# A first part of 144 rows streamed as 192 columns in tiles of its own, in a fused attention, routing and expert kernel

## The chip, the core and the metric

The kernel runs on one core of a Trainium2 chip. A core has five engines that run side by side and meet only at semaphores: PE (TensorE, the matmuls; PEld is its weight load, which overlaps the matmuls), DVE (VectorE), ACT (ScalarE), POOL (GpSimd) and SP (SyncE, which here issues most of the transfers). The metric is the device time of one execution in microseconds. Before the change it is 773.58 us, the median of 3 runs (773.41 to 774.14). PE's clock has two levels, 2.4 GHz (granted clock 1.00) and 1.2 GHz (0.50), and the profile gives the granted clock of each stretch.

## The reference

Three pieces follow each other. Attention: 4 batches, 8 heads, 576 tokens of width 64, a pooled attention over groups of 4 tokens plus a local one over a band of 7 tokens. Its output, 2304 tokens of width 512, goes through a routed layer, and that one's output through a last layer of width 2048:

```
logits = x @ w_gate;  expert_idx = argmax(logits, axis=1)
for e in range(8):                      # w1[e]: 512 x 1024, w2[e]: 1024 x 512
    h = maximum(x[expert_idx == e] @ w1[e], 0)
    out[expert_idx == e] = gate_w * (h @ w2[e])
h = out @ w_in                          # 512 x 2048
g = where(h >= 1, h, where(h <= -1, 0, (h + 1)**2 / 4))
return g @ w_out                        # 2048 x 512
```

All of it is float32 in and out.

## The kernel before

**Precision.** A float32 operand of the two big layers is split into a high part (rounded to the type fp32r) and a low part (the rest). Each product is then three passes: high by high, low by high, high by low. `whi` makes the high part of a block of weights on ACT (names wraw to wh), `wlo` the low part (wl) on DVE or POOL. Activations are split the same way into xh and xl, hidden values into hh and hl.

**Attention and routing.** The steps of this part are written out by hand in the string ORDER: each word names a step (S, AV, xt, ...) with its numbers, and the loop at L785 emits them one after the other, which fixes the order on every engine. At its end tokens are routed in chunks of 128-row groups (CHUNKS): `lg` the logits, `ct` a transpose of them, `ch` the argmax on DVE (it writes oh_all, the one-hot choice), `gt` the gate, `ra`/`rk`/`rd` a token's place in its expert's list (PE adds up one-hot rows; dst_all is the place). `xt` transposes 128 tokens back to rows, `xm` scales them on ACT or DVE into one of four buffers xr, and `xs` scatters them with POOL to their expert's rows in the DRAM tensor xs_d.

**Slots.** The experts are handled in 8 slots, by their number of tokens, the fullest first; slot s has a capacity CAPS[s] (416 for slot 0). For eight steps f, `emit_p1` makes 128 hidden rows from the slot's tokens (12 matmuls, weights stationary, tokens streamed as columns), and `emit_p2` adds their share to four output banks y0 to y3 (12 matmuls). A block of 512 KB of weights serves two steps; eight blocks make a slot. Blocks come through 4 raw buffers (wraw), so a load waits until an earlier block is split.

**The first slot is started early.** After 9 of the 18 groups, `pick` (L652) chooses the expert that is fullest so far. `ld_rows` (step xa) then reads its first NA = 128 rows from xs_d while routing still goes on. Step XA.0 transposes them on PE, XA.1 casts them to xh on ACT, XA.2 makes xl on DVE. Steps wh.0 to wh.2 make the high parts of the slot's first three blocks, wqp.0, wqv.1 and wqv.2 their low parts (p on POOL, v on DVE), and wl.0 to wl.5 issue the loads of six blocks. With these rows alone, part A runs the first FA = 6 steps of slot 0. Part B runs the same steps for the columns from NA on, in two forms that the program chooses between by the token count: to column 416, or to NARROW[0] = 352 when the expert has no more. The inputs take the second. Then steps 6 and 7 run over all columns. Before A, `clear` zeroes PSUM banks with matmuls against a zero column, because A and B write different columns of the same bank.

**Beside A.** `count` adds up the one-hot rows on PE for the tokens per expert. `tables` (13 small DVE operations and two count matmuls) turns them into the slots' experts and counts, `starts` (8 DVE operations, after A's second step) and `positions` (4, after the third) into places in the output. Each iteration of the loop over `seq` ends with the split of the next weight block if WFIRST allows it (after the second, third and fourth step: blocks 3, 4 and 5). After the fourth step comes a branch (`emit_overflow`, not taken here), and `load_n` reads the count of slot 0 into a register of PE. `load_rest` (L839) reads the rest of slot 0's rows, after the last scatter. `x_rest` (L1036) transposes and splits them, half before and half after A's last `emit_p2`.

PSUM banks of the routing part are taken from a list by `take` in the order in which they were given back.

Of the kernel before, what the change touches and what calls it, by code (L numbers as in the profile page):

```python
# [32 lines left out]
CAP = 384  # L33
# [5 lines left out]
NWB, NWC, NWR = 3, 4, 4  # L39
NA, GA, FA, TOP = 128, 3, 6, 4096  # L40
NWT = NWB + NWC
# [45 lines left out]
nmv.11 voa.3.1 xt.10 cx.3 gt.3 aca.9.0 ap.9.0 AV.9.1 xt.9 rk.3 xt.11 tr.11 AV.10.0 aca.9.1 ap.9.1 rd.3 lg.4 xma.10  # L87
AV.10.1 xmv.9 ad.10.0 bda.11.0 xma.11 bdv.11.2 bdv.11.1 loa.4 bda.11.3 wh.0 wh.1 ct.4 ra.4 xs.10 ad.10.1 ch.4 cx.4 xt.12 xt.13 lg.5 XA.0 rk.4 gt.4 xs.11 AV.11.1 AV.11.0 rd.4 xs.9 wqp.0 wl.2 wl.3 xma.13 XA.1 loa.5 ad.11.1 ct.5 ad.11.0 xt.14 ch.5 wqv.1 wl.4 lg.6 ra.5 xma.12 wh.2 loa.6
xma.14 ct.6 rk.5 rd.5 xs.13 xt.15 cx.5 ra.6 ta gt.5 xt.17 xs.12 xs.14 xma.15 xt.16 ch.6 xs.15 cx.6 gt.6 XA.2 wl.5 rk.6 rd.6
xma.16 xma.17 xs.16 xs.17 wqv.2  # L90
"""
# [29 lines left out]
def body(ctx: ExitStack, tc: tile.TileContext, qT, kT, kD, vS, wg, w1, w2, w_in, w_out, cst, out, dbg=None, parts="all"):  # L121
# [547 lines left out]
    def next_pools():  # L669
        early.close()  # L670
        P["hp"] = pool(ctx, "hp", 3, "left")
        wC.extend(pool(ctx, f"wC{i}", NWC, "left") for i in range(2))
        P["xp"], P["xq"] = pool(mctx, "xp", 1, "left"), pool(mctx, "xq", 1, "left")

    P = {}

    def ld_rows():

        first["xr"] = P["xp"].tile([128, 4, DM], F32, tag="xr2", name="xr2")
        i_ = SP.dma_start(out=first["xr"][:, 0, :], in_=xs_d[bass.ds(sp_exp[0] * ROWS, NA), :])  # L680
        early_rows.append(i_)

    def xa_(k):
        if k == 0:
            p_ = first["p"] = take("xa")
            for c in range(4):
                PE.transpose(out=p_[:, NA * c:NA * c + NA], in_=first["xr"][:, 0, 128 * c:128 * c + 128], identity=ident)
            first["x"] = [[P["xq"].tile([128, CAPS[0]], F32R, tag=f"x{t}{c}", name=f"x{t}{c}") for t in "hl"] for c in range(4)]
        for c, (hi, lo) in enumerate(first["x"]):
            src = first["p"][:, NA * c:NA * c + NA]  # L690
# [4 lines left out]
        if k == 2:  # L695
            give("xa")

# [11 lines left out]
    def count(a, b):  # L709
        n_ps = T["n"] = T["n"] if a else take("n")  # L710
        for g in range(a, b):
            PE.matmul(out=n_ps[:, 0:E], lhsT=onesb, rhs=oh_all[:, g, :], start=(g == 0), stop=(g == NR - 1))
# [126 lines left out]
    def load_rest():  # L839
        last = SP.value_load(last_i[0:1, 0:1], min_val=0, max_val=E * ROWS - 128)  # L840
        xr, m = first["xr"], (CAPS[0] - 128 - NA) // 2
        SP.dma_start(out=xr[0:m, 1:3, :], in_=xs_d[bass.ds(sp_exp[0] * ROWS + NA, 2 * m), :].rearrange("(t p) d -> p t d", p=m))
        SP.dma_start(out=xr[:, 3, :], in_=xs_d[bass.ds(last, 128), :])

# [325 lines left out]
    for k, (v, f) in enumerate(seq):  # L1170
        if k == FA - 1:
            xb = x_rest()
            next(xb)
            emit_p2(v, f, hl, yb)
            next(xb)
            hln = emit_p1(*seq[k + 1], xhl)
        elif k + 1 < len(seq):
# [17 lines left out]
        elif k == 2:  # L1195
# [201 lines left out]
```

## Time and profile before

| | |
|---|---|
| median of 3 runs | 773.58 us |
| the profiled execution, own time | 781.72 us |
| its span, first to last instruction | 780.0 us |
| granted clock, mean over the span | 0.967 |
| PE busy | 753.1 us (97%) |
| DVE, ACT, POOL busy | 526.3, 341.3, 257.4 us |
| part A's first product to part B's start | 122.0 to 157.7 us |

The profile is of one execution, which took 8.1 us more than the median of the runs without a profile. A busy engine in it is one with an instruction in flight, so PE's 97% is not 97% of its peak. Idle time is listed with the engine that ended it.

### The profile page before, as it was taken

The page shows a single profiled execution, that of the slowest core. Times are in us where ns is not written, and L with a number is a line of the kernel's source. Part 1 is how long each engine was busy: PE and PEld are TensorE (multiplying, and loading weights), DVE is VectorE, ACT ScalarE, POOL GpSimd, SP SyncE. Part 2 cuts the span into 40 slices and gives each one's busy share as a digit, 9 for nine tenths or more (in the row PEclk, how much of TensorE's full clock was granted, in tenths as well). Part 3 has the DMA queues.
Part 4 walks back from the last instruction along what each step waited for, and adds up shares of the span by engine and source line. Part 5 has one row for each costly group of instructions (what it writes and reads, how often), then busy time and mean ns, then how long its engine had stood idle before and what let it go on. Part 6 is the DMA issues. An engine that isn't in the chain of part 4 may idle for free.

```text
span 780.0 us, 14586 instructions
## 1 busy us (share of the span) xinstructions
PE 753.1 (97%) x5667; PEld 681.5 (87%) x5668; DVE 526.3 (67%) x908; ACT 341.3 (44%) x709; POOL 257.4 (33%) x243
## 2 busy tenths in 40 slices
PE   4799989999999999999999999999999999999996
PEld 2567668999999999999999899999899899899896
DVE  5879965366466877875676676676876868744444
ACT  1767773145354565554454544333333333322221
POOL 5536653000014334300275733333323333221113
PEclk9989996589999999999999999999999999999999
DMA  9879256236456655763001011010101000011112
GB/s 287 233 245 308 96 183 214 84 118 188 152 165 218 214 191 202 243 218 110 28 28 55 28 54 54 29 55 28 55 28 55 30 25 1 1 41 40 41 42 81
DMA packets 47833, 87.11 MB, mean 112 GB/s; under 512 B 3100, under 2 KB 23964, under 8 KB 47752
## 3 DMA queue, kind: packets, MB, share of 16 engines
q1 hardware_dynamic: 44872, 76.56, 30.5%
q0 software_dynamic: 2880, 9.44, 3.2%
q8 instruction: 55, 0.90, 0.5%
q14 instruction: 26, 0.21, 0.1%
HBM read 76.55 MB, written 9.44 MB: 110 GB/s over the span
## 4 chain that ended last, share of the span: by engine, by line
PE 72%; issue 5%; POOL 2%; ACT 1%; DVE 1%; DMA 1%; POOLq 0%; SPq 0%; ACTq 0%; PEldq 0%
PE s L1136 23%; PE y L1282 15%; PE y L1086 13%; PE s L1069 12%; PE o L1282 8%; POOL out_dram L1302 1%; PE o L1022 1%; DMA xr<-xs_d 1%; ACT wh L181 0%; PE o L1042 0%; DVE wl L185 0%; POOLq L1392 0%; POOL gap_t L1304 0%; DVE hl L1009 0%; ACT hh L1008 0%
## 5 line engine op out<-in xcount | busy, mean ns | idle before, releaser
L1136 PE MATMUL s<-yT,wh 128*128 128x384 f32 x448 | 140.4, 336 | 0.0
L965 POOL TENSOR_SCALAR cvm<-cvm 128x512 f32<-128x512 f32 x32 | 52.8, 1650 | 245.6 <-ACT cvm L964 245.1
L1148 ACT CAST hh<-r 128x384 fp32r<-128x384 f32 x95 | 48.8, 513 | 161.3 <-DVE r L1144 161.3
L1143 DVE SCALAR_TENSOR_TENSOR r<-r 128x384 f32<-128x384 f32 x96 | 61.6, 642 | 64.7 <-ACT r L1142 63.2
L1142 ACT ACTIVATE r<-s,half 128x384 f32<-128x384 f32 x96 | 55.7, 580 | 87.5 <-PE s L1136 87.3
L1149 DVE TENSOR_TENSOR hl<-r,hh 128x384 fp32r<-128x384 f32 x95 | 56.4, 593 | 55.1 <-ACT hh L1148 54.0
L185 DVE TENSOR_TENSOR wl<-wraw,wh 128x1024 fp32r<-128x1024 f32 x63 | 79.6, 1279 | 18.0 <-ACT wh L181 17.3
L1136 PEld LDWEIGHTS s<-yT,wh 128*128 128x128 f32 x448 | 83.5, 188 | 4.6
L1136 PE MATMUL s<-yh,wh 128*128 128x384 f32 x256 | 86.3, 337 | 0.0
L1136 PE MATMUL s<-yh,wl 128*128 128x384 f32 x256 | 86.2, 337 | 0.0
L940 POOL TENSOR_TENSOR wl<-cvm,wh 128x512 fp32r<-128x512 f32 x32 | 51.0, 1594 | 98.5 <-ACT wh L939 87.5
L1086 PE MATMUL y<-hh,wh 128*128 128x240 f32 (+7 forms) x280 | 80.5, 309 | 0.0
L1086 PE MATMUL y<-hh,wl 128*128 128x240 f32 (+7 forms) x280 | 79.3, 304 | 0.0
L1008 ACT ACTIVATE hh<-s 128x288 fp32r<-128x288 f32 (+8 forms) x70 | 28.9, 413 | 104.1 <-PE s L1069 103.0
L1282 PE MATMUL y<-wl,hh 128*128 128x512 f32 x189 | 74.4, 393 | 0.0
L1282 PE MATMUL y<-wh,hh 128*128 128x512 f32 x189 | 73.8, 390 | 0.0
L1009 DVE SCALAR_TENSOR_TENSOR hl<-s,hh 128x288 fp32r<-128x288 f32 (+8 forms) x70 | 32.0, 457 | 58.2 <-ACT hh L1008 57.8
L181 ACT CAST wh<-wraw 128x1024 fp32r<-128x1024 f32 x64 | 65.5, 1045 | 5.4 <-issue 3.6
L1282 PE MATMUL y<-wh,hl 128*128 128x512 f32 x189 | 59.2, 392 | 0.0
L1086 PEld LDWEIGHTS y<-hh,wl 128*128 128x128 f32 x280 | 56.4, 201 | 0.0
L1086 PEld LDWEIGHTS y<-hh,wh 128*128 128x128 f32 x280 | 56.4, 201 | 0.0
L1144 DVE TENSOR_TENSOR r<-s,r 128x384 f32<-128x384 f32 x96 | 53.5, 557 | 3.3
(321 smaller groups left out, 1677.0 us busy)
## 6 DMA issues: line engine op xcount, KB each, us to landing
wraw<-in_dram SPq DMA_DIRECT2D x88, 512.0 KB
v_s<-in_dram SPq DMA_DIRECT2D x12, 512.0 KB
kbd<-in_dram SPq DMA_DIRECT2D x16, 296.0 KB
kraw<-in_dram SPq DMA_DIRECT2D x4, 1152.0 KB
craw<-in_dram SPq DMA_DIRECT2D x8, 512.0 KB
q_t<-in_dram SPq DMA_DIRECT2D x4, 768.0 KB
xr<-xs_d SPq DMA_DIRECT2D x10, 256.0 KB
q_t<-in_dram SPq DMA_DIRECT2D x4, 400.0 KB
```

The lines of the kernel that those rows point to most:

```text
L181: ACT.copy(out=hi, in_=raw)
L185: eng.tensor_tensor(out=lo, in0=raw, in1=hi.bitcast(F32), op=ALU.subtract)
L940: POOL.tensor_tensor(out=lo, in0=m, in1=hi.bitcast(F32), op=ALU.subtract)
L965: POOL.tensor_scalar(out=m, in0=m, scalar1=PAT_MIN * PAT_MIN, scalar2=None, op0=ALU.is_ge)
L1069: PE.matmul(out=h_ps[:, b:m], lhsT=w[wi][:, o:o + 128], rhs=xhl[c][xi][:, b:m], start=(n == 0), stop=(n == 11))
L1086: PE.matmul(out=y_ps[c][:, b:m], lhsT=w[wi][:, o:o + 128], rhs=hl[xi][:, b:m], start=(f == 0 and i == 0 and v not in ("A", "B")), stop=(f ...
L1136: PE.matmul(out=h_ps[:, 0:CAP], lhsT=w[wi][:, o:o + 128], rhs=yhl[j, c][xi], start=(n == 0), stop=(n == 11))
L1142: ACT.activation(out=r, in_=h_ps[:, 0:CAP], func=AF.Relu, scale=0.5, bias=half[:, 0:1])
L1143: DVE.scalar_tensor_tensor(out=r, in0=r, scalar=1.0, in1=r, op0=ALU.min, op1=ALU.mult)
L1144: DVE.tensor_tensor(out=r, in0=h_ps[:, 0:CAP], in1=r, op=ALU.max)
L1149: DVE.tensor_tensor(out=lo[:, 0:CAP], in0=r, in1=hi[:, 0:CAP].bitcast(F32), op=ALU.subtract)
L1282: PE.matmul(out=p, lhsT=gl[gi][:, 128 * t:128 * t + 128], rhs=w[wi][:, o + c:o + c + p.shape[-1]], start=(f % 4 == 0 and i == 0), stop=(f ...
```

## The change

Part A takes 144 rows instead of 128 (NA) and streams 192 columns (NZ). The 48 columns behind the rows are zeros, written once by POOL. A's operands no longer lie in the tiles of slot 0 (`first["x"]`) but in four tiles hi0 of 384 columns, one half for the high and one for the low part (`first["xa"]`). These tiles existed already for a later use and now come from another pool, allocated earlier. After A's third step ACT and POOL copy the 144 columns into `first["x"]`, for steps 6 and 7. Part B has 272 columns, or 208 in the narrow form (before 288 and 224).

The 144 rows are read as two tiles of 72 rows, so XA.0 has eight transposes of 72 columns in two PSUM banks, where it had four of 128 in one. The rest is two tiles of 72 rows and the last 128 rows.

In ORDER, wh.0 comes earlier, and the low part of block 0 moves from POOL to DVE (wqp.0 to wqv.0) to an earlier place. XA.1 and XA.2 move ahead, wqv.1 behind the routing of the last chunk, and the low part of block 2 (wqv.2) leaves ORDER and stands behind `tables` in the program. `count` takes its bank by preference from o0, o1 and s0.

```
-NA, GA, FA, TOP = 128, 3, 6, 4096
+NA, NZ, GA, FA, TOP = 144, 192, 3, 6, 4096
...
-AV.10.1 xmv.9 ad.10.0 bda.11.0 xma.11 bdv.11.2 bdv.11.1 loa.4 bda.11.3 wh.0 wh.1 ct.4 ...
+AV.10.1 xmv.9 ad.10.0 bda.11.0 xma.11 bdv.11.2 bdv.11.1 wh.0 wqv.0 loa.4 bda.11.3 wh.1 ct.4 ...
...
-    def take(*key):
-        held[key] = free.pop(0)
+    def take(*key, first=()):
+        held[key] = free.pop(min((free.index(t) for t in first if t in free), default=0))
...
         P["hp"] = pool(ctx, "hp", 3, "left")
+        hi0.extend(P["hp"].tile([128, CAP], F32R, tag=f"hi0{c}", name=f"hi0{c}", bufs=1) for c in range(4))
...
-        i_ = SP.dma_start(out=first["xr"][:, 0, :], in_=xs_d[bass.ds(sp_exp[0] * ROWS, NA), :])
+        i_ = SP.dma_start(out=first["xr"][0:NA // 2, 0:2, :],
+                          in_=xs_d[bass.ds(sp_exp[0] * ROWS, NA), :].rearrange("(t p) d -> p t d", p=NA // 2))
...
+            first["xa"] = [[hi0[c][:, i * NZ:i * NZ + NZ] for i in range(2)] for c in range(4)]
...
+            for hl in first["xa"]:
+                for t in hl:
+                    POOL.memset(t[:, NA:].bitcast(F32), 0.0)
             for c in range(4):
-                PE.transpose(out=p_[:, NA * c:NA * c + NA], in_=first["xr"][:, 0, 128 * c:128 * c + 128], identity=ident)
+                if c % 2 == 0:
+                    first["p", c // 2] = take("xa", c // 2)
+                for t in range(2):
+                    o = NA * (c % 2) + m * t
+                    PE.transpose(out=first["p", c // 2][:, o:o + m], in_=first["xr"][0:m, t, 128 * c:128 * c + 128], identity=ident[0:m, 0:m])
...
-        n_ps = T["n"] = T["n"] if a else take("n")
+        n_ps = T["n"] = T["n"] if a else take("n", first=("o0", "o1", "s0"))
...
-        return (0, 0, NA, 0) if v == "A" else (0, NA, CAPS[0], NARROW[0]) if v == "B" else (v, 0, CAPS[v], NARROW[v])
+        return (0, 0, NZ, 0) if v == "A" else (0, NA, CAPS[0], NARROW[0]) if v == "B" else (v, 0, CAPS[v], NARROW[v])
...
-    xhl = first["x"]
+    xhl = first["xa"]
...
     tables()
+    wd_(DVE, 2)
     hb[0] = bank("s0")
...
             next(xb)
+            xhl = first["x"]
             hln = emit_p1(*seq[k + 1], xhl)
...
             flag = nc.values_load(flag_i[0:1, 0:1], min_val=0, max_val=NT)
+            for c in range(4):
+                for i, copy in enumerate((ACT.copy, POOL.tensor_copy)):
+                    copy(out=first["x"][c][i][:, 0:NA], in_=first["xa"][c][i][:, 0:NA])
```

How this stands on PE where A begins: the two last matmuls of the count (onesb against oh_all, L712 before and L722 after), then the clearing of bank s (zerob) and of the first y bank, then A's second product. Before:

```order
500 L712 MATMUL y_2019<-oh_all,onesb 128x8
501 L712 LDWEIGHTS onesb
502 L712 MATMUL y_2019<-oh_all,onesb 128x8
503 L1157 LDWEIGHTS onesb
504 L1157 MATMUL s_2129<-zerob,onesb 128x416
505 L1157 LDWEIGHTS onesb
506 L1157 MATMUL y_2131<-zerob,onesb 128x416
```

and now:

```order
501 L722 MATMUL o_2039<-oh_all,onesb 128x8
502 L722 LDWEIGHTS onesb
503 L722 MATMUL o_2039<-oh_all,onesb 128x8
504 L1166 LDWEIGHTS onesb
505 L1166 MATMUL s_2146<-zerob,onesb 128x416
506 L1166 LDWEIGHTS onesb
507 L1166 MATMUL y_2148<-zerob,onesb 128x416
```

The count now lies in an o bank, so that no clearing of a y bank follows it in its own bank.

On DVE, from the end of the routing of the last chunk through `tables` (key, cnt_bc, ... flag_i; rows between are left as they were) stood before:

```order
222 L619 TENSOR_TENSOR rk<-s_2001,oh_all 128x16
223 L621 TENSOR_REDUCE dst_all<-rk 128x2
224 L185 TENSOR_TENSOR wl<-wraw,wh 128x1024
225 L1009 SCALAR_TENSOR_TENSOR hl<-s_2091,hh 128x128
226 L718 SCALAR_TENSOR_TENSOR key<-y_2019,keyb 128x8
```

and behind flag_i there are now, before the split of A's second and third hidden rows (hl):

```order
237 L747 TENSOR_REDUCE flag_i<-fl 1x1
238 L185 TENSOR_TENSOR wl<-wraw,wh 128x1024
239 L1018 SCALAR_TENSOR_TENSOR hl<-s_2146,hh 128x192
240 L1018 SCALAR_TENSOR_TENSOR hl<-s_2107,hh 128x192
241 L185 TENSOR_TENSOR wl<-wraw,wh 128x1024
242 L753 TENSOR_TENSOR gtr<-key 128x64
```

The subtraction of block 2 (row 224 before) has moved behind the 13 operations of `tables` (row 238).

On POOL, between two scatters (xs_d) of the routing, stood before:

```order
65 L644 MEMSET gap_t 1x1
66 L185 TENSOR_TENSOR wl<-wraw,wh 128x1024
67 L171 MEMSET wraw 128x1
68 L642 DMA xs_d<-xr,dst_all 20480x512
69 L644 MEMSET gap_t 1x1
```

and now:

```order
69 L644 MEMSET gap_t 1x1
70 L171 MEMSET wraw 128x1
71 L642 DMA xs_d<-xr,dst_all 20480x512
72 L644 MEMSET gap_t 1x1
73 L642 DMA xs_d<-xr,dst_all 20480x512
```

The subtraction of block 0 (row 66 before) is gone from POOL.

## Rows read from the trace of the kernel before

**Rows 1.** The page: span, and granted clock in 40 equal slices.

```profile
span 780.0 us, 14586 instructions
...
PEclk9989996589999999999999999999999999999999
```

**Rows 2.** Stretches; us busy of PE, PEld, DVE, ACT, POOL; granted clock; transfers.

```profile
114.80:118.20 3.40, 3.40 (x37) 2.55 (x33) 2.02 (x9) 2.81 (x8) 2.11 (x4) 0.50 0.94 257
118.20:125.00 6.80, 5.82 (x90) 4.78 (x83) 5.63 (x25) 3.39 (x8) 2.88 (x5) 1.00 0.94 332
125.00:157.70 32.70, 31.50 (x148) 30.71 (x148) 9.73 (x32) 5.15 (x11) 3.53 (x11) 0.50 0.32 101
157.70:162.60 4.90, 4.90 (x25) 4.84 (x24) 1.37 (x3) 1.04 (x3) 0.00 (x0) 0.50 0.00 0
162.60:174.90 12.30, 12.30 (x112) 12.30 (x111) 10.74 (x20) 6.75 (x10) 0.00 (x0) 1.00 0.53 174
```

**Rows 3.** Waits of PE, 108 to 175 us: total, times, longest.

```profile
PE y L612 <- DVE oh_all L588: 1.5, 1, 1.5
```

**Rows 4.** Timeline of PE where A begins: start, duration (us), what.

```profile
125.03 1.55 PE L1157 MATMUL y<-zerob,onesb 128*128 128x416 bf16 x4 [0.79 <-DVE cnt_bc L720]
126.10 1.23 PE L1069 MATMUL s<-xh,wh 128*128 128x128 f32 x4
127.12 1.05 PE L1069 MATMUL s<-xl,wh 128*128 128x128 f32 x4
127.98 1.05 PE L1069 MATMUL s<-xh,wl 128*128 128x128 f32 x4
```

**Rows 5.** The same timeline, from A's branch into part B and beyond.

```profile
145.90 1.05 PE L1086 MATMUL y<-hl,wh 128*128 128x128 f32 x4
148.12 1.10 PE L1069 MATMUL s<-xh,wh 128*128 128x128 f32 x4 [1.16 <-PEq L872]
...
157.71 1.31 PE L1069 MATMUL s<-xh,wh 128*128 128x224 f32 x4
158.82 1.05 PE L1069 MATMUL s<-xh,wl 128*128 128x224 f32 x4
159.68 1.05 PE L1069 MATMUL s<-xl,wh 128*128 128x224 f32 x4
...
164.20 0.61 PE L1069 MATMUL s<-xh,wh 128*128 128x224 f32 x4
...
165.54 0.27 PE L1086 MATMUL y<-hh,wh 128*128 128x224 f32 x1
...
183.44 0.79 PE L1022 MATMUL o<-ident,xr 120*128 120x120 f32 x6
183.99 0.41 PE L1086 MATMUL y<-hh,wh 128*128 128x352 f32 x1
```

**Rows 6.** Timeline of POOL, 104 to 160 us.

```profile
110.95 2.35 POOL L185 TENSOR_TENSOR wl<-wraw,wh 128x1024 fp32r<-128x1024 f32 x1
```

**Rows 7.** Timeline of DVE, 108 to 160 us.

```profile
112.18 1.17 DVE L582 TENSOR_TENSOR lgx<-l,rmx 128x24 f32<-128x24 f32 x1
...
124.75 0.15 DVE L718 SCALAR_TENSOR_TENSOR key<-y,keyb 128x8 f32<-128x8 f32 x1
...
126.69 0.16 DVE L737 TENSOR_REDUCE flag_i<-fl 1x1 int32<-1x16 f32 x1
...
135.43 1.23 DVE L185 TENSOR_TENSOR wl<-wraw,wh 128x1024 fp32r<-128x1024 f32 x1 [0.64 <-ACT wh L181]
136.57 0.22 DVE L743 TENSOR_TENSOR gtr<-key 128x64 f32<-128x64 f32 x1
...
137.86 0.15 DVE L755 CAST caps_i<-cs 1x8 int32<-1x8 f32 x1
```

**Rows 8.** Timeline of ACT, 108 to 160 us.

```profile
123.67 0.68 ACT L767 ACTIVATE xr<-o,gt 128x512 f32<-128x512 f32 x1
```

**Rows 9.** By stretch, after the loads of slot 0's remaining rows.

```profile
134.00:135.00 1.00, 1.00 (x6) 1.00 (x6) 0.29 (x1) 0.81 (x2) 0.00 (x0) 0.50 0.00 0
```

More of the change, by code (lines that the diff above doesn't have):

```diff
@@ L87 @@
 nmv.11 voa.3.1 xt.10 cx.3 gt.3 aca.9.0 ap.9.0 AV.9.1 xt.9 rk.3 xt.11 tr.11 AV.10.0 aca.9.1 ap.9.1 rd.3 lg.4 xma.10
-AV.10.1 xmv.9 ad.10.0 bda.11.0 xma.11 bdv.11.2 bdv.11.1 loa.4 bda.11.3 wh.0 wh.1 ct.4 ra.4 xs.10 ad.10.1 ch.4 cx.4 xt.12 xt.13 lg.5 XA.0 rk.4 gt.4 xs.11 AV.11.1 AV.11.0 rd.4 xs.9 wqp.0 wl.2 wl.3 xma.13 XA.1 loa.5 ad.11.1 ct.5 ad.11.0 xt.14 ch.5 wqv.1 wl.4 lg.6 ra.5 xma.12 wh.2 loa.6
-xma.14 ct.6 rk.5 rd.5 xs.13 xt.15 cx.5 ra.6 ta gt.5 xt.17 xs.12 xs.14 xma.15 xt.16 ch.6 xs.15 cx.6 gt.6 XA.2 wl.5 rk.6 rd.6
-xma.16 xma.17 xs.16 xs.17 wqv.2
+AV.10.1 xmv.9 ad.10.0 bda.11.0 xma.11 bdv.11.2 bdv.11.1 wh.0 wqv.0 loa.4 bda.11.3 wh.1 ct.4 ra.4 xs.10 ad.10.1 ch.4 xt.12 xt.13 lg.5 XA.0 XA.1 cx.4 rk.4 gt.4 xs.11 AV.11.1 AV.11.0 rd.4 xs.9 wl.2 wl.3 xma.13 loa.5 ad.11.1 ct.5 ad.11.0 xt.14 ch.5 XA.2 wl.4 lg.6 ra.5 xma.12 wh.2 loa.6
+xma.14 ct.6 rk.5 rd.5 xs.13 xt.15 cx.5 ra.6 ta gt.5 xt.17 xs.12 xs.14 xma.15 xt.16 ch.6 xs.15 cx.6 gt.6 wqv.1 wl.5 rk.6 rd.6
+xma.16 xma.17 xs.16 xs.17
 """
@@ L671, in next_pools @@
         P["hp"] = pool(ctx, "hp", 3, "left")
+        hi0.extend(P["hp"].tile([128, CAP], F32R, tag=f"hi0{c}", name=f"hi0{c}", bufs=1) for c in range(4))
         wC.extend(pool(ctx, f"wC{i}", NWC, "left") for i in range(2))
         P["xp"], P["xq"] = pool(mctx, "xp", 1, "left"), pool(mctx, "xq", 1, "left")
-    P = {}
+    P, hi0 = {}, []
     def ld_rows():
         first["xr"] = P["xp"].tile([128, 4, DM], F32, tag="xr2", name="xr2")
-        i_ = SP.dma_start(out=first["xr"][:, 0, :], in_=xs_d[bass.ds(sp_exp[0] * ROWS, NA), :])
+        i_ = SP.dma_start(out=first["xr"][0:NA // 2, 0:2, :],
+                          in_=xs_d[bass.ds(sp_exp[0] * ROWS, NA), :].rearrange("(t p) d -> p t d", p=NA // 2))
         early_rows.append(i_)
     def xa_(k):
+        m = NA // 2
         if k == 0:
-            p_ = first["p"] = take("xa")
-            for c in range(4):
-                PE.transpose(out=p_[:, NA * c:NA * c + NA], in_=first["xr"][:, 0, 128 * c:128 * c + 128], identity=ident)
-            first["x"] = [[P["xq"].tile([128, CAPS[0]], F32R, tag=f"x{t}{c}", name=f"x{t}{c}") for t in "hl"] for c in range(4)]
-        for c, (hi, lo) in enumerate(first["x"]):
-            src = first["p"][:, NA * c:NA * c + NA]
+            first["xa"] = [[hi0[c][:, i * NZ:i * NZ + NZ] for i in range(2)] for c in range(4)]
+            first["x"] = [[P["xq"].tile([128, CAPS[0]], F32R, tag=f"x{t}{c}", name=f"x{t}{c}") for t in "hl"] for c in range(4)]
+            for hl in first["xa"]:
+                for t in hl:
+                    POOL.memset(t[:, NA:].bitcast(F32), 0.0)
+            for c in range(4):
+                if c % 2 == 0:
[3 more added lines that the diff above has]
+                    PE.transpose(out=first["p", c // 2][:, o:o + m], in_=first["xr"][0:m, t, 128 * c:128 * c + 128], identity=ident[0:m, 0:m])
+        for c, (hi, lo) in enumerate(first["xa"]):
+            src = first["p", c // 2][:, NA * (c % 2):NA * (c % 2) + NA]
             if k == 1:
@@ L694, in xa_ @@
                 DVE.tensor_tensor(out=lo[:, 0:NA], in0=src, in1=hi[:, 0:NA].bitcast(F32), op=ALU.subtract)
-        if k == 2:
-            give("xa")
+                if c % 2:
+                    give("xa", c // 2)
     def wh_(i):
@@ L841, in load_rest @@
         xr, m = first["xr"], (CAPS[0] - 128 - NA) // 2
-        SP.dma_start(out=xr[0:m, 1:3, :], in_=xs_d[bass.ds(sp_exp[0] * ROWS + NA, 2 * m), :].rearrange("(t p) d -> p t d", p=m))
-        SP.dma_start(out=xr[:, 3, :], in_=xs_d[bass.ds(last, 128), :])
+        SP.dma_start(out=xr[0:m, 2:4, :], in_=xs_d[bass.ds(sp_exp[0] * ROWS + NA, 2 * m), :].rearrange("(t p) d -> p t d", p=m))
+        SP.dma_start(out=xr[:, 0, :], in_=xs_d[bass.ds(last, 128), :])
     def load_x(s):
@@ L888, in rest_pools @@
         yp = pool(ctx, "yp", 1, "right")
-        hi0.extend(yp.tile([128, CAP], F32R, tag=f"hi0{c}", name=f"hi0{c}") for c in range(4))
         yT.extend(yp.tile([128, YCOLS], F32, tag=f"yT{c}", name=f"yT{c}") for c in range(4))
@@ L895, in inner_pools @@
         wB.append(pool(mctx, "wB", NWB, "right"))
-    hi0, yT = [], []
+    yT = []
     wide = w_in.dtype != F32
@@ L1040, in x_rest @@
             p_ = next_bank("o")
-            for t, c0, k in ((3, 0, 128), (1, 128, m), (2, 128 + m, m)):
+            for t, c0, k in ((0, 0, 128), (2, 128, m), (3, 128 + m, m)):
                 PE.transpose(out=p_[:, c0:c0 + k], in_=xr[0:k, t, 128 * c:128 * c + 128], identity=ident[0:k, 0:k])
```

## The prediction

> **What bounds the kernel now.** I read the page first. Its line of the granted clock [rows 1] shows full speed nearly everywhere, and a dip between slices 6 and 9, some 114 to 163 us into the span of 780.0 us. The view by stretch [rows 2] puts numbers to it. PE is busy for 31.5 of the 32.7 us from 125.0 to 157.7 us, which is part A, yet its clock is 0.50, that is 1.2 GHz. DVE is busy for 9.7 us there, ACT for 5.2, POOL for 3.5, and the transfers take a third. So no engine and no transfer limits A; it is long because PE's clock is halved. Part B begins at the same half clock, which comes back 4.9 us later, at 162.6 us, and stays.
>
> The timeline gives the pace. At the half clock four matmuls of 128 columns take 0.86 us (127.12 to 127.98 [rows 4]), and four of 224 columns also take 0.86 us (158.82 to 159.68 [rows 5]): 0.215 us each for either width. At full clock twelve of 224 columns take 1.34 us (164.20 to 165.54 [rows 5]), 0.112 each. A matmul of up to 224 columns is thus bound by something that does not depend on its columns, and 192 columns cost what 128 cost.
>
> The clock fell twice. At 114.8 us [rows 2] it fell after PE had waited 1.5 us for oh_all [rows 3]; at 118.2 it was back. It fell again at 125.0, after PE had waited 0.79 us for cnt_bc [rows 4], with little but matmuls of 128 and 8 columns before. After that, 128 columns never raised it in 32.7 us, while B's 224 did in 4.9. No row has 192. This is the open point on which the time hangs.
>
> **The change, part by part.** The sum is made against the profiled execution, 781.72 us; the median without a profile is 773.58, 8.1 less, and I take the difference over to it unchanged.
>
> *Before A.* The wait for oh_all ends a chain of small DVE operations. One of them, L582, took 1.17 us [rows 7], where others of a like size take 0.15 to 0.16; it ran while POOL made block 0's low part, 110.95 to 113.30 [rows 6], and ended 0.05 us behind it. The change takes this subtraction off POOL. On DVE it costs 1.23 us [rows 7], in a place where DVE is idle. The gain is at most 1.0 us. Against it stands wh.0, now ahead of the copy that the chain's transposes need; if its transfer is late the chain is too, so the bounds are -0.3 and 1.0, and I take 0.7, near the row. The eight zeroings on POOL stand behind a scatter, in the 2.3 us that the subtraction leaves.
>
> *The clearing.* The y banks no longer wait for cnt_bc. Next in line is ACT's last scaling of routed rows out of such a bank, which ends at 123.67 + 0.68 = 124.35 [rows 8]. So of the wait until 125.03 some 0.6 us goes (0 to 0.8). The four clearings take 1.07 us at the half clock (125.03 to 126.10 [rows 4]); at full clock I put 0.55, a gain of 0.5. A's second product would start at 126.10 - 0.7 - 0.6 - 0.5 = 124.3.
>
> *Part A at full clock.* From A's second product to B's first, 126.10 to 157.71 [rows 4, 5], is 31.6 us. It holds five products of emit_p1 and six of emit_p2, 132 matmuls. At full clock these are 132 x 0.112 = 14.8 us. Twelve transposes of the rest are 1.1 (six take 183.44 to 183.99 [rows 5]). The branch costs 1.4: the last four matmuls before it, from 145.90, are through at 146.76, and PE resumes at 148.12 [rows 5]. Two waits are added that the half clock hid:
>
> First, DVE. A step becomes 24 x 0.112 = 2.7 us. After `tables` (2.1 us, from 124.75 to 126.85 [rows 7], now 0.7 earlier) DVE has block 2's low part, 1.23, done at about 127.5. A's third product starts at 124.3 + 2.7 = 127.0 and uses that part in its last four matmuls, from 127.9: in time. Then come in turn a split of hidden values, 1.23 for block 3, the eight operations of `starts` (1.4 us, 136.57 to 138.01 [rows 7]), and only then the next split and 1.23 for block 4. Steps three and four of A give DVE 2.7 us each, and it has about 3.0 and 3.0 to do, behind a start that is 1 us late: block 4 is done at about 135.0, and PE wants it for the last four matmuls of the fifth product, at 133.7. That is a wait of 1.3, and 0.2 more for block 3. I take 1.5. The bounds are 0, where all hides, and 4, the 1.4 of `starts` and two of the 1.23 fully in the open.
>
> Second, the casts behind the last transposes. B's first four matmuls took 1.11 us instead of 0.86 [rows 5], 157.71 to 158.82, since ACT was still casting. The casts take as long as before, the four matmuls only 0.45, so the wait is 0.7.
>
> The sum is 14.8 + 1.1 + 1.4 + 1.5 + 0.7 = 19.5, a gain of 12.1.
>
> *Part B.* From 157.71 to 164.20 [rows 5] it had 36 matmuls in 6.5 us; at full clock they are 4.0, a gain of 2.5. Its 208 columns are below 224, so they gain nothing more.
>
> *Nothing.* The 64 added columns per matmul, 144 times: at 0.215 for 128 and 224 alike, 0; were they paid in proportion, 0.215 x 64 / 128 x 144 = 15.5 us at the half clock and 7.7 at full. I take 0, the row nearer to it. [...] The eight copies into `first["x"]` lie on ACT and POOL, which have 5.2 and 3.5 us of work in 32.7; uncovered, four of 144 columns on ACT would be less than four scalings of 512, 4 x 0.68 = 2.7 us [rows 8]. The rest of slot 0's rows have arrived by 134.0 (the transfers are silent after it [rows 9]); x_rest would start near 138, so a cover of 4 us remains. Weight blocks 3 to 5 are loaded before A, and B keeps its pace.
>
> Together 0.7 + 0.6 + 0.5 + 12.1 + 2.5 = 16.4: 781.72 becomes 765.3, and the median 773.58 becomes **757.2 us**.
>
> **The rivals.**
>
> *The clock is full for a part of A only* (it starts low and rises, or falls at the 1.4 us of the branch). A step at half clock takes 24 x 0.215 = 5.2 us instead of 2.7, so two to five such steps cost 5 to 12: 762 to 769, centre 765. For it: A still begins behind waits. Against it: after 118.2 the clock held through a stretch with 5.8 of 6.8 us busy in small matmuls [rows 2].
>
> *192 columns do not raise it and A starts low.* Then A keeps its 31.6 us, B raises the clock as before, and only the waits ahead of A go: 0.7 + 0.6, so 772.3. For it: 128 columns did nothing in 32.7 us, and 192 lie between them and 224.
>
> *B loses it as well: slower.* It was B's 224 columns that brought the clock back. If neither 192 nor 208 do, the half clock lasts until step 6 of slot 0 with its 352 columns. B's six steps, 144 matmuls, then cost 144 x (0.215 - 0.112) = 14.8 us more than at full clock, of which 2.5 are paid already: 773.58 - 1.3 + 12.3 = 784.6. It decides if the clock is low when A begins, and a stretch of 208 columns, unlike the row's 224, leaves it low. Against it: 208 differ little from 224, and PE need only stay at full clock from before.
>
> *The added columns are paid* at full clock, 757.2 + 7.7 = 765. The equal pace of 128 and 224 speaks against it.
>
> **How the numbers follow.** The forecast (full clock from A's first products or soon after) gets 0.66; its own range is 754 to 761, from the bounds of the DVE waits, the two gains before A, and one step at half clock. The clock for a part of A gets 0.13, low in A 0.13, low in B too 0.06, paid columns 0.02. The range of 753 to 772.5 holds nearly all of the first, second and last and half of the third. A measurement of this kernel tells 0.2%, 1.5 us, from no change, so faster is below 772.0. The third case straddles that: 0.04 of it counts as faster and 0.09 as the same. Faster 0.66 + 0.13 + 0.02 + 0.04 = 0.85, same 0.09, slower 0.06.
>
> **What would show it.** In the changed kernel's profile the granted clock should be 1.00 from A's first products through B, 12 matmuls of 192 columns should take 1.34 us, and from A's second product to B's first should be near 19.5 us. The wait for cnt_bc should be gone, one for an ACT scaling in its place; L582 should take 0.2 us; PE should wait for a low part (wl) after A's third step. The forecast is wrong if the clock in A is 0.50 (third case), wrong on the slow side if it is still 0.50 in B after some 5 us, and mis-sized if PE waits on DVE or for x_rest's transfer by more than 4 us.

## The result, and the profile after

The changed kernel takes 767.86 us, the median of 20 runs (764.60 to 773.12); 20 runs of the kernel before, taken beside them, have a median of 774.77. A ratio, here and below, is taken between the means of the two kernels' runs, without those over 1.5% above their kernel's fastest. Here it is 0.9886 (95% interval 0.9856 to 0.9917). The forecast was 757.2 us: the change gained some 6.9 us on the medians, where 16.4 were expected. The time lies where the first rival put it, a clock that is full for a part of A only. One profiled execution after took 768.84 us at a mean granted clock of 0.988, against 781.72 us at 0.967.

The page's span and granted clock, as in [rows 1]:

```profile
span 767.1 us, 14608 instructions
...
PEclk9999998899999999999999999999999999999999
```

The dip is smaller, not gone. The stretches with their clock, as in [rows 2] (us busy of PE, PEld, DVE, ACT, POOL; granted clock; transfers):

```profile
117.50:123.80 6.30, 6.30 (x62) 5.83 (x61) 3.00 (x14) 2.06 (x4) 3.53 (x7) 0.50 0.79 273
124.00:140.90 16.90, 13.77 (x116) 13.08 (x115) 9.93 (x33) 5.29 (x13) 4.43 (x13) 1.00 0.60 187
141.00:147.50 6.50, 6.50 (x36) 6.50 (x35) 1.32 (x4) 1.31 (x5) 0.00 (x0) 0.50 0.00 0
147.80:175.00 27.20, 27.09 (x216) 26.77 (x215) 20.09 (x39) 13.23 (x26) 0.00 (x0) 1.00 0.53 166
```

A's first product starts at half clock, at 120.8 us; the rest of A's first four steps runs at 1.00; then the clock is 0.50 again until B's start. PE's timeline, the rows that answer to [rows 4, 5]:

```profile
121.91 1.05 PE L1078 MATMUL s<-hi,wl 128*128 128x192 f32 x4
122.76 1.06 PE L1078 MATMUL s<-hi,wh 128*128 128x192 f32 x4
...
123.73 0.38 PE L1166 MATMUL s<-zerob,onesb 128*128 128x416 bf16 x1
123.95 0.87 PE L1166 MATMUL y<-zerob,onesb 128*128 128x416 bf16 x4
124.51 1.18 PE L1078 MATMUL s<-hi,wh 128*128 128x192 f32 x8
...
125.98 0.27 PE L1095 MATMUL y<-hh,wh 128*128 128x192 f32 x1
...
127.32 1.06 PE L1078 MATMUL s<-hi,wh 128*128 128x192 f32 x8
...
134.18 0.69 PE L1078 MATMUL s<-hi,wl 128*128 128x192 f32 x4 [0.19 <-DVE wl L185]
...
135.60 0.61 PE L1095 MATMUL y<-hl,wh 128*128 128x192 f32 x4
139.16 1.13 PE L1078 MATMUL s<-hi,wh 128*128 128x192 f32 x8 [2.94 <-PEq L882]
140.13 0.61 PE L1078 MATMUL s<-hi,wl 128*128 128x192 f32 x4
...
147.16 1.10 PE L1078 MATMUL s<-xh,wh 128*128 128x208 f32 x4
```

The waits for oh_all [rows 3] and for cnt_bc [rows 4] are gone, and no wait for an ACT scaling came in their place. A's second product starts at 124.51, where the working put 124.3. From there to B's first product it is 22.65 us; it was 31.61, and 19.5 were expected. The largest wait is 2.94 us at A's branch, where PE's sequencer (PEq) is named; before it was 1.16 [rows 5]. Behind it the clock falls.

What the sequencer did there is in the view by source line, for the line of the branch (duration in ns, shortest/median/longest, then first and last start in us; PEldq is PE's sequencer, SPq is SP's; EVENT_SEMAPHORE is a step at which the engines meet):

```profile
L807 PEldq EVENT_SEMAPHORE  x2: 51/51/51, 138.1 to 138.3; - x2
...
L807 PEldq COMPARE_BRANCH  x1: 3831/3831/3831, 134.2 to 134.2; - x1
...
L807 SPq COMPARE_BRANCH  x1: 53/53/53, 137.9 to 137.9; - x1
```

PE's jump over the body of the branch took 3.83 us. It was issued at 134.2; the matmuls already handed to PE covered it until 136.21 (135.60 + 0.61). Beside it stand transfers of program code (the view of the transfers, 134 to 138 us: packets, MB, share):

```profile
q1 hardware_dynamic: 671, 0.81, 62.6%
q8 instruction: 1, 0.02, 2.8%
q14 instruction: 3, 0.02, 1.5%
```

By its record in the trace the one on q8 runs from 135.2 to 137.0; the jump ends at 138.1. In the kernel before a transfer on q8 follows the branch too, but it begins at 144.6, when the jump (142.9, 0.38 us) is over.

### The profile page after: what moved, and what is told of

The parts are those of the page before. It is cut to its first block, busy times and chain, and to the rows that moved or that the text cites. A ratio compares the mean times of both kernels' runs of the same rounds, so it can differ in the third digit from the quotient of the medians.

```text
span 767.1 us, 14608 instructions
## 1 busy us (share of the span) xinstructions
PE 740.6 (97%) x5671; PEld 669.6 (87%) x5672; DVE 526.5 (69%) x909; ACT 342.1 (45%) x713; POOL 257.4 (34%) x254
## 4 chain that ended last, share of the span: by engine, by line
PE 72%; issue 5%; POOL 2%; ACT 1%; DVE 1%; DMA 1%; POOLq 0%; SPq 0%; ACTq 0%; PEldq 0%
PE s L1145 23%; PE y L1296 15%; PE y L1095 13%; PE s L1078 12%; PE o L1296 8%; POOL out_dram L1316 1%; PE o L1031 1%; DMA xr<-xs_d 1%; ACT wh L181 0%; PE o L1051 0%; DVE wl L185 0%; POOLq L1406 0%; POOL gap_t L1318 0%; DVE hl L1018 0%; ACT hh L1017 0%
## 5 line engine op out<-in xcount | busy, mean ns | idle before, releaser
L1095 PE MATMUL y<-hh,wh 128*128 128x240 f32 (+7 forms) x280 | 77.5, 300 | 0.0
L1095 PE MATMUL y<-hh,wl 128*128 128x240 f32 (+7 forms) x280 | 76.3, 296 | 0.0
L1017 ACT ACTIVATE hh<-s 128x272 fp32r<-128x272 f32 (+8 forms) x70 | 29.1, 416 | 93.6 <-PE s L1078 93.6
L1018 DVE SCALAR_TENSOR_TENSOR hl<-s,hh 128x272 fp32r<-128x272 f32 (+8 forms) x70 | 32.3, 461 | 50.1 <-ACT hh L1017 46.9
L1095 PEld LDWEIGHTS y<-hh,wl 128*128 128x128 f32 x280 | 54.0, 193 | 0.0
L1095 PEld LDWEIGHTS y<-hh,wh 128*128 128x128 f32 x280 | 53.9, 193 | 0.0
```

The lines of the kernel that those rows point to most:

```text
L1095: PE.matmul(out=y_ps[c][:, b:m], lhsT=w[wi][:, o:o + 128], rhs=hl[xi][:, b:m], start=(f == 0 and i == 0 and v not in ("A", "B")), stop=(f ...
```

## The experiments

Two questions were open. Where did the forecast's gain go? My theory was that it is half-clock time, left in A and already missing in the median runs of before; the rival was that the gain is waits and order, and the clock has little to do with it. And what makes PE idle at the branch: the transfers under way (H1), the copies ahead of it (H2) or, later, where the jump lands (H3)?

**1. The kernel before again**, unchanged.

> The kernel before, unchanged, so that each of its runs has its granted clock beside its time. Theory 1 (half-clock time is the missing gain): the profiled execution of before, 781.72 us at a mean clock of 0.967, was one with long half-clock stretches; runs near 773.6 should show a clock near 0.980 (8.1 us over the slope of about 615 us per 1.0 of clock that the 20 runs of the changed kernel have), so a part of the forecast's gain lay in the median already. Rival (the profile costs 8 us of its own): the clock is 0.967 at 773.6 us too.

Twelve runs, 773.26 to 787.14 us. The five with a mean clock of 0.963 to 0.969 took 781.6 to 787.1, the seven with 0.978 to 0.986 took 773.3 to 779.1. Longer runs have the lower clock, and runs without a profile are as long: so the 8.1 us between the profiled execution and the median go with half-clock time. Theory 1 holds, the rival is out. Its profile fell on the longest run (787.14); its stretches:

```profile
104.00:119.50 15.50, 11.71 (x177) 8.55 (x172) 12.65 (x34) 9.09 (x20) 9.58 (x14) 1.00 0.66 211
120.00:163.50 43.50, 41.91 (x225) 40.17 (x226) 15.30 (x56) 8.78 (x19) 6.41 (x15) 0.50 0.36 118
```

and its jump at the same branch:

```profile
L797 PEldq COMPARE_BRANCH  x1: 382/382/382, 146.1 to 146.1; - x1
```

The same branch cost PE's sequencer 0.38 us in the old order, a tenth.

**2. The added columns alone**, in the kernel before.

```
-NA, GA, FA, TOP = 128, 3, 6, 4096
+NA, NZ, GA, FA, TOP = 128, 192, 3, 6, 4096
+            for hl in first["x"]:
+                for t in hl:
+                    POOL.memset(t[:, NA:NZ].bitcast(F32), 0.0)
-        return (0, 0, NA, 0) if v == "A" else ...
+        return (0, 0, NZ, 0) if v == "A" else ...
```

> The kernel before with one part of the change: A streams 192 columns, 128 rows and 64 zeros, in the old tiles, in the old order, with the old waits. Theory 1 (the width of the stream raises the clock): A still starts low behind the wait for cnt_bc, the clock rises to 1.00 within A, and the time is 765 to 770 us; twelve matmuls of 192 columns take 2.6 us while the clock is 0.50 and 1.34 at 1.00. Rival A (the gain comes from the waits that the new places of conversions and counts took away): the time stays within 1.5 us of before's and the clock in A is 0.50. Rival B (added columns are paid): slower than before by 4 to 8 us.

772.11 us (12 runs, 768.57 to 774.48), ratio 0.9959 (0.9929 to 0.9989). The columns aren't paid (rival B is out), the clock in A is not 0.50 (rival A is out), and none of its runs is of the kind near 785 us. The profile shows full clock in most of A:

```profile
124.00:140.00 16.00, 13.32 (x113) 12.37 (x111) 9.96 (x33) 5.28 (x10) 4.09 (x10) 1.00 0.58 171
140.50:143.50 3.00, 3.00 (x16) 3.00 (x16) 0.12 (x1) 0.33 (x1) 0.24 (x1) 0.50 0.53 182
```

The profiled run, 768.57, lies in the forecast band of 765 to 770, the median two us above it. The low stretch in the second row follows the branch, where PE is idle for 2.04 us; the jump there took 0.37 us.

**3. The changed kernel without the zeros.**

```
-NA, NZ, GA, FA, TOP = 144, 192, 3, 6, 4096
+NA, NZ, GA, FA, TOP = 144, 144, 3, 6, 4096
```

> The changed kernel without the 48 added columns of zeros: A streams its 144 rows as 144 columns, all else as changed. Theory 1: the clock that A needs comes from the width, so it is 0.50 for most of A, A's second product to B's first takes near 31 us as before and not 22.65, and the time is 772 to 777 us. Rival A (waits and order are the gain): within 1.5 us of the changed kernel, 767.9. Rival B (columns are paid): faster than the changed kernel by 2 to 4 us.

770.28 us (12 runs), ratio 0.9918 (0.9879 to 0.9957): theory 1 as written fails. Rival A doesn't fit either, since the time is 2.4 us above the changed kernel's 767.86, though the two did not run side by side. The stretches:

```profile
104.00:135.50 31.50, 28.55 (x350) 24.31 (x345) 23.83 (x87) 17.71 (x40) 14.76 (x30) 1.00 0.77 253
136.00:152.50 16.50, 15.63 (x76) 15.60 (x77) 2.62 (x7) 2.77 (x8) 0.23 (x1) 0.50 0.11 35
```

With 144 columns the clock held at 1.00 through A's start and four of its steps. Then PE was idle for 3.09 us at the branch, the clock fell, and it stayed at 0.50 for 16.5 us and more, into B; in the changed kernel, with 192 columns, that was 6.5 us and more (141.0 to 147.5). So the width is not needed to keep the clock up; it brings it back sooner. The idle time at the branch is what the two have in common.

**4. The copies into first["x"] behind the branch.**

```
         elif k == 3:
             emit_overflow(flag, yT)
             inner_pools()
             load_n(0)
+            for c in range(4):
+                for i, copy in enumerate((ACT.copy, POOL.tensor_copy)):
+                    copy(...)          # moved from k == 2
```

> The changed kernel with the eight copies of A's operands into first[x] moved from ahead of the branch to behind it. Theory H2 (POOL's and ACT's copies delay PE's way past the branch): PE's idle time there falls from 2.94 us (named PEq L882) to some 1.2 to 1.5, the clock stays at 1.00 behind it, and the time is 762 to 765 us. Theory H1 (the weight blocks' loads, which are under way at the branch, delay it): the idle time stays 2.5 to 3 us, the clock falls behind it again, and the time stays within 1.5 us of 767.9. If instead the copies come too late for the seventh step, PE waits for first[x] at its start by 1 to 3 us.

769.00 us (12 runs), ratio 0.9903 (0.9869 to 0.9937). The jump got longer:

```profile
L807 PEldq COMPARE_BRANCH  x1: 5611/5611/5611, 132.1 to 132.1; - x1
```

PE was idle for 4.80 us, and the clock fell. H2 is out: it isn't the copies.

**5. No branch**, and so no path for an expert with more tokens than its slot holds.

```
-            flag = nc.values_load(flag_i[0:1, 0:1], min_val=0, max_val=NT)
-            emit_overflow(flag, yT)
```

> The changed kernel without the branch behind A's fourth step (the path for an expert with more tokens than its slot holds is left out; these inputs don't take it). Theory: the branch is what takes the rest of the gain, by PE's idle 2.94 us there and by the half clock that follows it from 140.95 to about 147.7 us, 3.4 us more. Without it PE has no idle time there, the clock stays at 1.00 into part B, A's second product to B's first is 19.5 to 20.5 us instead of 22.65, and the time is 767.9 - 2.9 - 3.4 = 761.5 us, 759 to 763. Rival (the gap only moves: PE then waits for a low part on DVE or for the rest of the rows): idle time of 2 to 4 us in the next two steps, the clock falls there, and the time is 765.5 to 768.

763.76 us (6 runs, 762.27 to 765.29), ratio 0.9875 (0.9845 to 0.9904). Less was gained than worked out (761.5), but the steps are as the theory has them:

```profile
120.00:123.30 3.30, 3.30 (x18) 2.67 (x17) 1.78 (x7) 1.62 (x3) 1.53 (x5) 0.50 0.52 174
123.50:140.00 16.50, 16.32 (x145) 16.03 (x144) 10.48 (x31) 5.99 (x14) 4.71 (x13) 1.00 0.65 202
140.00:175.00 35.00, 34.41 (x258) 33.45 (x256) 24.19 (x44) 16.67 (x31) 0.00 (x0) 1.00 0.53 163
```

No idle time takes the branch's place, the clock holds into B, and A's second product to B's first is 16.57 us (123.49 to 140.06), less than the 19.5 to 20.5 expected. The profiled executions are 6.2 us apart (768.84 and 762.68), near the 6.3 worked out (2.9 + 3.4), the medians 4.1. Kernels 6 and 7 below ran on the same chip beside it, with the branch's idle time of the changed kernel: the one without the branch is 4.2 and 4.7 us faster.

**6. The loads behind the branch.**

```
-            next_wt()
+            next_wt(k not in (1, 2, 3))     # no load_wt() in these
...
             load_n(0)
+            for _ in range(3):
+                load_wt()
```

> The changed kernel with the loads of the three weight blocks that are under way at the branch issued behind it. Theory H1 (PE's jump over the body of the branch has to fetch code, and the weight blocks' transfers hold the fetch up): PE's jump, 3.83 us in the changed kernel, takes under 2 us, PE is idle for 1.0 to 2.0 us instead of 2.94, and the time is 764 to 766.5 us. Rival (the fetch takes its time whatever else is transferred, or PE waits for SP, which reaches the branch late behind its loads): the jump stays at 3.5 to 5.6 us with the loads away, the idle time at 2.5 us or more, and the time within 1.5 us of 767.9; if it was SP, the idle time falls but the jump's length does not.

767.97 us (9 runs), ratio 0.9929 (0.9898 to 0.9959); jump 3.88 us, idle 3.01. This can't be read for H1, since the loads did not become late. SP passed the branch before PE reached it (134.2), and the three went out at 132.6, 134.1 and 137.4; in the changed kernel three go out at 131.4, 134.2 and 137.5:

```profile
L808 SPq COMPARE_BRANCH  x1: 53/53/53, 131.3 to 131.3; - x1
```

```profile
132.56 5.23 SPq L172 DMA_DIRECT2D wraw<-in_dram  x3
```

It rules out the other half of the rival: SP's late arrival, 137.9 in the changed kernel, isn't what PE waits for.

**7. The same, with the count loaded earlier** (load_n(0) moved from k == 3 to k == 2, ahead of the load of the flag).

> As the one before (loads behind the branch), and the load of slot 0's count into a register of PE moved from behind the branch to A's third step. Theory: that load and what follows it, 138.34 to 139.16 us in the changed kernel, stand in the open behind the jump; moved, the idle time is 0.7 to 0.9 us shorter than with the loads alone, 0.3 to 1.3 us in all, short enough that the clock may hold, and the time is 761.5 to 765. Rival (PE's sequencer waits for the fetch in any case, and the load is hidden in it): the idle time is that of the loads alone, and so is the time within 1 us.

768.41 us (6 runs), ratio 0.9916 (0.9884 to 0.9947); jump 4.74 us, idle 3.09. PE goes on 0.3 us behind the jump's end instead of 1.1, but the jump was longer by as much. The rival holds.

**8. No branch and no zeros** (the edits of 3 and 5).

> Without the branch (the path for an expert with more tokens than its slot holds is left out), and A's 144 rows streamed as 144 columns, without the zeros. Theory (the width only brings a fallen clock back, it does not keep it up): with no idle time to lower it the clock stays at 1.00 through A with 144 columns as well, and the time is within 2 us of the kernel without the branch. Rival (A needs 192 columns to hold the clock): it falls within A, 144 columns don't raise it, and the time is 5 to 12 us above that of the kernel without the branch.

766.72 us (6 runs), ratio 0.9878 (0.9838 to 0.9919). Four runs took 761.69 to 767.49, and the ratio is theirs; two took 780.11 and 781.50 at mean clocks of 0.967 and 0.971. The profile is of a short one: the clock fell ahead of A, and came back while 144 columns were streamed.

```profile
119.50:129.00 9.50, 9.50 (x75) 8.28 (x73) 5.35 (x29) 2.53 (x7) 4.24 (x9) 0.50 0.51 182
129.50:145.00 15.50, 15.34 (x139) 15.08 (x139) 8.33 (x23) 5.89 (x15) 3.83 (x10) 1.00 0.55 171
```

Neither side is right alone. 144 columns can do nearly as well as 192 (the shortest run is 761.69, against 762.27 in 5); but the median is 3.0 us above 5's, and two of six runs lost 13 us or more, which no run with 192 columns in the new order did. No profile was taken of such a run.

**What was left: where the jump lands.** The jump took 0.37 to 0.38 us in the kernel before and in 2, and 3.8 to 5.6 us in every kernel with the branch and the new XA.0. This has four more transposes on PE, each with its weight load: eight instructions more ahead of the branch. So I took eight away elsewhere, and in another kernel added 132.

**9. Eight instructions fewer** (the first four warming steps at the program's start have one matmul instead of two).

```
-        for _ in range(n):
+        nwarm[0] += 1
+        for _ in range(1 if nwarm[0] <= 4 else n):
             PE.matmul(out=w_ps, lhsT=onesb, rhs=...)
```

> The changed kernel with four warming matmuls fewer at its very start, so that PE's program ahead of the branch is 8 instructions shorter, as long as before's. Theory H3 (where PE's jump lands decides: in before and in the kernel with added columns alone the landing lies in the piece of program that PE has already fetched, in the changed kernel 8 instructions further on, just behind its end): PE's jump takes 0.37 to 0.4 us instead of 3.83. Only a handful of instructions are left in that piece behind the landing, so PE is still idle for 1.9 to 2.2 us, as with the added columns alone, and the time is 765.5 to 768.5 us. Rival (the jump waits for transfers or for another engine): it takes 3.8 to 5.6 us as in all five kernels with the new order, and PE is idle for 2.9 to 4.8 us.

764.97 us (4 runs, 762.89 to 765.69). The jump, and then PE's timeline behind it:

```profile
L810 PEldq COMPARE_BRANCH  x1: 373/373/373, 131.0 to 131.0; - x1
```

```profile
135.30 1.26 PE L1081 MATMUL s<-hi,wh 128*128 128x192 f32 x8 [2.35 <-issue]
```

3.83 us became 0.37, with the weight blocks' loads where they were (SP's jump at 134.6). PE was still idle for 2.35 us, now named issue, a little more than the 1.9 to 2.2 expected (the time is a little less). The jump is past; what is missing is the program behind it, as in 2. The records of the transfers fit that: one on q8 runs from 132.9 to 133.8, and PE goes on at 135.30, 1.5 us behind its end. In 2 it is 1.2 us (139.0 to 140.26), and the long jumps end 1.0 to 1.6 us behind theirs. The rival is out, and with it H1 as the cause.

**10. 132 instructions more** (the first 22 warming matmuls of 512 columns as four of 128 each).

```
+        if nwarm[0] <= 11:
+            for q in range(4 * n):
+                PE.matmul(out=w_ps[:, 128 * (q % 4):128 * (q % 4) + 128], lhsT=onesb, rhs=onesb, ...)
```

> The changed kernel with the first 22 warming matmuls of 512 columns each made as four of 128, 132 instructions more on PE ahead of the branch. Theory H3: the landing then lies well inside the piece that is fetched ahead, with some 120 instructions left behind it; the jump takes under 0.5 us, PE is idle for 1.0 to 1.4 us (the load of the count behind the jump, as in before), and the time is 763 to 766.5 us. Rival (position doesn't matter): jump of 3.8 us or more, idle time of 3 us, 767 to 769 us.

765.34 us (6 runs, 763.12 to 767.98).

```profile
L814 PEldq COMPARE_BRANCH  x1: 368/368/368, 135.6 to 135.6; - x1
```

```profile
138.58 1.13 PE L1085 MATMUL s<-hi,wh 128*128 128x192 f32 x8 [1.06 <-PEq L889]
```

The idle time is 1.06 us, as worked out, and the clock stays at 1.00 behind it. PE goes on before the transfer on q8 (137.4 to 139.3) has ended.

**11. The same, with the count loaded earlier.**

> As the one before, and the load of slot 0's count into a register of PE moved from behind the branch to A's third step. Theory H3: with the landing fetched nothing but the meeting of the engines is left, PE is idle for 0.2 to 0.6 us, the clock holds through A and B, and the time is that of the kernel without the branch within 1.5 us, 762 to 765.5 us, below both the kernel before and the changed one. Rival: the jump stays long, idle 3 us as with the earlier load alone, 767 to 769 us.

764.06 us (6 runs, 761.96 to 766.49).

```profile
137.58 1.11 PE L1085 MATMUL s<-hi,wh 128*128 128x192 f32 x8 [0.30 <-PEq L814]
```

```profile
121.00:124.00 3.00, 3.00 (x17) 2.93 (x16) 1.98 (x7) 1.35 (x3) 1.08 (x3) 0.50 0.51 180
124.50:142.50 18.00, 17.53 (x154) 16.77 (x153) 11.08 (x36) 6.32 (x15) 5.55 (x15) 1.00 0.67 206
```

The branch is kept and costs 0.30 us; A to B is 17.02 us (125.59 to 142.61). It has the lowest median of the versions that compute all of the reference, 3.8 us below the changed kernel's. But none of 9 to 11 ran beside the changed kernel, and the ranges overlap, so what the landing is worth in time is not shown as its idle time is. (The ratios of 9 to 11, 0.981, 0.982 and 0.980, say little: eight of the eleven runs of before beside them took 783 to 786 us.)

**12. ACT's cast of block 2 later** (in 11; wh.2 moved in ORDER from behind xma.12 to behind xma.17).

What is left low is the stretch ahead of A. In the changed kernel and in 10, ACT's cast of block 2 waits for the block's transfer. In the changed kernel:

```profile
115.31 1.04 ACT L181 CAST wh<-wraw 128x1024 fp32r<-128x1024 f32 x1 [0.87 <-DMA wraw<-in_dram]
```

and in 10:

```profile
116.01 1.04 ACT L181 CAST wh<-wraw 128x1024 fp32r<-128x1024 f32 x1 [2.92 <-DMA wraw<-in_dram]
```

> The kernel with the landing inside the fetched piece and the earlier load of the count, and ACT's high part of block 2 (the third of its casts of 128x1024) moved behind the last scaling of routed rows. Theory: what is left of the half clock, from 117 to 124 us, comes from that cast: it waits on ACT for the block's transfer (0.87 us in the changed kernel's profile, 2.17 and 2.92 in the last two kernels', nothing in the kernel without the branch), and the copy lp behind it keeps PE waiting for as long. Moved, PE's wait for lp near 117 us is under 0.5 us in any execution, A begins at 1.00, and the time is 760 to 763 us, with the runs within 3 us of each other. Rival (another wait takes its place: oh_all, the count, or the low part of block 2, now later): PE waits 0.5 us or more between 116 and 128 us, the clock falls at A's start all the same, and the time is that of the kernel before this one, 762 to 766.5.

765.19 us (6 runs, 764.07 to 767.49), ratio 0.9905 (0.9871 to 0.9938). The half clock is gone from the whole part, and the time is no better than 11's 764.06 (the two did not run side by side). Its stretch, and PE's waits from 100 to 200 us:

```profile
104.00:163.00 59.00, 56.23 (x596) 51.25 (x592) 41.18 (x124) 29.67 (x61) 15.89 (x40) 1.00 0.65 203
```

```profile
PE y L1173 <- ACT xr L784: 0.9, 1, 0.9
PE s L1085 <- DVE wl L185: 0.8, 2, 0.6
```

The rival holds in its waits and its time, not in the clock, which did not fall. PE waits for block 2's low part, which is now late, and at the clearing for ACT's last scalings, which wait for the buffers that earlier scatters read:

```profile
123.00 1.27 ACT L784 ACTIVATE xr<-y,gt 128x512 f32<-128x512 f32 x2 [2.63 <-DMA xs_d<-xr,dst_all]
```

These scalings end at about the same time in both, 124.27 in 12 and 124.09 in 11. In 11 PE came to this clearing at 125.03 and waited for nothing; in 12 it was there earlier and waited until 123.74. So part of the half clock ahead of A had covered a wait.

## Why the prediction was right and wrong

**Right.** Columns: twelve matmuls of 192 columns take 1.34 us at full clock (the product that begins at 125.98, to the next at 127.32), as 224 did [rows 5], and four take 0.85 us at half clock (121.91 to 122.76), as 128 did [rows 4]. The copies, the zeros and the rest of the rows cost nothing that PE's timeline shows. L582 fell from 1.17 us [rows 7] to 0.18:

```profile
110.81 0.18 DVE L582 TENSOR_TENSOR lgx<-l,rmx 128x24 f32<-128x24 f32 x1
```

Of the 1.8 us worked out ahead of A's second product, 1.6 came (126.10 to 124.51), but partly by luck. A's first product began 1.2 us earlier (122.03 to 120.83) instead of 0.7, and the clearing gave 1.4 instead of 1.1; the product itself, at half clock, took 1.0 us longer (1.82 to 2.79), which the sum had not.

**Wrong, first: the difference carried over to the median.** I took the profiled execution's 8.1 us above the median as a constant. Experiment 1 ties them to half-clock time, which is what the change was to take away: of the 14.6 us that I worked out for A and B at full clock, a run near the median no longer had all to give. Between the two profiles the gain is 12.9 us (781.72 to 768.84), and after, profile and median are 1.0 apart. This step cost 8.1 - 1.0 = 7.1 of the 10.7 us by which the forecast was low; the other 3.5 are the 16.4 us worked out less the 12.9. In which stretches a shorter run of before is at full clock isn't known, since both its profiles are of long runs. The working also has it that a difference of 0.2%, 1.5 us, can be told from none. The 20 runs of the kernel before alone spread over 11.7 us (773.34 to 785.00), and the interval of the ratio is 0.6% wide.

**Wrong, second: "The branch costs 1.4".** It was 2.94 us of idle time (3.1 counted as the 1.4 was, from 135.60 + 0.45 to 139.16), and it brought the clock down. I took the cost from the row as a property of the branch. Two parts have to be told apart. One is the meeting of the engines and the load of the count, which begin when PE has run dry:

```profile
L797 PEldq EVENT_SEMAPHORE  x2: 51/51/51, 147.0 to 147.1; - x2
```

This is the kernel before, where PE's last matmul ended at 146.95. No matmul covers this part, and it cost 1.16 us there at half clock and 1.06 at full (10), or 0.30 with the load moved ahead (11). The other is the jump and the code behind it, which the matmuls that PE had been given ahead do cover: at half clock these lasted 4.0 us from the jump on (in experiment 1's profile from 146.1 to 150.13, since PE went on at 151.29 after 1.16 idle), at full clock 2.0 us (134.2 to 136.21). And the jump itself went from 0.38 to 3.83 us, since eight more instructions stand ahead of it (9 and 10 show that it is the position). By these figures the longer jump would have fitted under the 4.0 us; of 2.0 it stuck out by 1.9. The Trainium skill (Runtime: NRT & Kernel Launch, section Instruction fetch mechanics) says that code is fetched ahead in order, in blocks of 256 instructions, and that a taken branch whose target isn't in the window that has been loaded has to wait for a fetch. The runs agree: 0.37 us or 3.83, with eight instructions between them, and long jumps that end behind a transfer of code on a queue of its own (q8). What a block holds is not shown here, beyond the 0.02 MB of that transfer.

In A's 22.65 us against 19.5, this is +1.7 at the branch and +3.1 for the 6.2 us of A at half clock behind it (141.0 to 147.16).

**Mis-sized: DVE and the casts.** The wait for low parts was 0.19 us, not 1.5. DVE's chain ran in the order listed, but from the start of block 3's low part to the end of block 4's it took 3.97 us, and block 4 was done at 134.1, not 135.0:

```profile
130.16 1.23 DVE L185 TENSOR_TENSOR wl<-wraw,wh 128x1024 fp32r<-128x1024 f32 x1 [0.58 <-ACT wh L181]
...
132.93 1.20 DVE L185 TENSOR_TENSOR wl<-wraw,wh 128x1024 fp32r<-128x1024 f32 x1
```

That gives 1.3 back. The 0.7 us for the casts should not stand in this sum, because that wait falls behind B's first product: B's first four matmuls took 0.94 us (147.16 to 148.10), and B's first 36 took 4.5 (to 151.66) instead of 4.0. So 19.5 + 1.7 + 3.1 - 1.3 - 0.7 = 22.3; the rest of the 22.65 has no named wait.

**The rivals.** The clock for a part of A only is what happened, for both of the reasons given: A started low, and the clock fell at the branch. It had 0.13; its place and its 765 were nearer than the forecast. 192 columns do raise the clock (in 2 from 0.50 to 1.00 by 144 us, with nothing but A's matmuls on PE; in the changed kernel by 124.0, behind A's first product), and B doesn't lose it.

**Open.** Why the jump into code that isn't loaded takes 3.8 us in one kernel and 5.6 in another. By the records of the transfers, the one on q8 begins 1.0 to 1.2 us after the jump in the changed kernel, 3, 6 and 7, and 2.8 us after it in 4; it lasts 1.3 to 1.8 us, in 7 2.1. So 4's jump fits a fetch that began late and 7's one that was slow, but why is not known. Open too are whether fewer transfers would shorten it (6 did not test that); and what the last low stretch, ahead of A, is worth by itself, since taking it away (12) brought 1.7 us of other waits.

## What to carry to other kernels

A wait in a profile can be what is left of a longer one behind the work that covers it: when the covering engine is to become twice as fast, work it out again from where the wait begins, and keep apart what no work covers. When a profiled execution is longer than the median, find out which of its stretches differ before carrying the difference over, above all when the change acts on those stretches. The branch of this unrolled program had a price that depended on where its landing lay, and eight instructions far ahead of it moved that by 3.5 us: look at the jump's own duration.

## What was not expected of the hardware

- The same jump takes 0.37 to 0.47 us (the kernel before, 2 and 9 to 12) or 3.83 to 5.61 us (the changed kernel, 3, 4, 6 and 7); eight instructions on the same engine ahead of it decide. On SP it takes 0.05 us in either case.
- An idle time of 2.94 us on PE was followed by more than 6 us at half clock, and 1.06 or 0.30 us at the same place by none (10, 11). Length alone doesn't decide: in the changed kernel the clock also fell at 117 us, behind a wait of 0.87 us that ended at 116.68.
- 144 columns held the clock at 1.00 for four steps of A (3), though 128 had not raised it in 32.7 us [rows 2].
